# Normalizing x tile by tile between attention slots, in a fused attention and gating kernel

## The chip, the cores and the metric

The kernel runs on one core of one Trainium2 chip. The metric is the device time of one execution in microseconds (us). Most executions agree within about 0.3%. Here the spread follows the mean clock that the chip granted to TensorE: in the 33 runs of the kernel before whose clock is on record, those at a mean clock of 0.989 to 0.991 of full speed (16 runs) had spans of 1152.2 to 1155.2 us, those at 0.994 to 0.996 (17 runs) had 1147.5 to 1150.8 us. Traces are therefore compared at equal clock where possible (all traced executions had 0.994 to 0.998), and some means below are over runs at a clock of 0.994 or more.

## The reference

```python
x = A_x                                  # 1 x 2048 x 640, bf16
xn = _layernorm(x)                       # (x - mean) / sqrt(var + eps)
s = attention(xn @ wq, k_cache[..., -512:, :], v_cache[..., -512:, :]) @ wo   # 32 heads of 192
# B: the two tokens with the largest r = xn @ w_r go through a small gated MLP,
#    scaled by sigmoid(r); the result is added to their rows of xn
g = silu(xn + scatter(y))
return x + s * g
```

The work is nearly all attention: 32 heads, 2048 queries, 512 keys. LayerNorm stands before everything, and the router (`r` for all 2048 tokens, then the best two) and the MLP of two tokens are small.

## The kernel before

The 32 heads are worked off in 16 pairs, and each pair in four slots of 512 queries. 2048 tokens are 16 tiles of 128 rows. `load_pair` starts the loads of one pair's keys, values and weights on the sync queue. First all 16 tiles of x are loaded, then all statistics are taken, then all tiles are normalized and transposed (`xnT` is what the q projection and the router read):

```python
x_all = lnp.tile([P, NT, D], BF16, name="x_all")
for t in range(NT):
    eng = nc.sync if t % 2 == 0 else nc.gpsimd
    eng.dma_start(out=x_all[:, t, :], in_=x2[t * P:(t + 1) * P, :])
loaded[0] = load_pair(0)
for t in range(NT):
    ...  # bn_stats, bn_aggr -> mv_all[:, t, :]
...      # rstd_all = 1 / sqrt(var + eps), one Sqrt for all tiles
for t in range(NT):
    nc.vector.tensor_scalar(out=xn_all[:, t, :], in0=x_all[:, t, :], scalar1=mv_all[:, t, 0:1],
                            scalar2=rstd_all[:, t:t + 1], op0=ALU.subtract, op1=ALU.mult)
    for d0 in range(0, DT, 4):
        ...
        pst = ps_a.tile([P, 4, P], BF16, name="pst", tag="ps_a")        # ps_a: two PSUM buffers
        for dt in range(dn):
            nc.tensor.transpose(pst[:, dt, :], xn_all[:, t, ...], ident[:])
        nc.any.tensor_copy(out=xnT[:, d0:d0 + dn, t * P:(t + 1) * P], in_=pst[:, :dn, :])
```

The router and the MLP are stages that are hung into the slots of attention, one stage a slot. Stage 1 is the router: 20 matmuls, then a chain of single-row operations on VectorE.

```python
def b_stage1():
    ...  # r_ps[1, 512] = wr_col^T @ xnT, 4 x 5 matmuls, copied to r_row
    r_bf = bw.tile([1, S], BF16, name="r_bf")
    nc.vector.tensor_copy(out=r_bf[:], in_=r_row[:])
    r_rt = bw.tile([1, S], F32, name="r_rt", tag="rowB")
    nc.vector.tensor_copy(out=r_rt[:], in_=r_bf[:])
    nc.vector.max(out=mx8[:], in_=r_rt[:])
    nc.vector.max_index(out=idx8[:], in_max=mx8[:], in_values=r_rt[:])
    ...
# stage 2: one-hot selectors E and ET; 3: the two rows; 4: gate and up (w_c, 24 loads); 5: down (wd_c)
def b_stage_g(c):                       # 16 of these, four a slot
    g_ps = ps_y.tile([P, 2, 512], F32, name="y_ps2")
    for nh in range(2):
        nc.tensor.matmul(g_ps[:, nh, :NH], lhsT=ident_h[:], rhs=xn_all[:, c, ...], start=True, stop=False)
        nc.tensor.matmul(g_ps[:, nh, :NH], lhsT=B.ET[:, c * P:(c + 1) * P], rhs=B.y_sb[:, ...],
                         start=False, stop=True)
    ...  # tanh on ScalarE, g = (tanh + 1) * g_ps on VectorE, written over xn_all

for i, st in enumerate(stages):
    b_sched.setdefault(slots[min(i, len(slots) - 1)], []).append(st)
```

Of the kernel before, what the change touches and what calls it, by code (L numbers as in the profile page):

```python
# [11 lines left out]
F32 = mybir.dt.float32  # L12
BF16 = mybir.dt.bfloat16
U32 = mybir.dt.uint32
I32 = mybir.dt.int32
# [4 lines left out]
def kernel(  # L20
# [15 lines left out]
    nc = tc.nc  # L36
    P = 128
    _, S, D = A_x.shape
# [5 lines left out]
    NT = S // P  # L44
# [4 lines left out]
    NQC = S // QC  # L49
    QPC = QC // P  # L50
# [7 lines left out]
    x2 = A_x[0]  # L58
    out2 = out[0]

    const = ctx.enter_context(tc.tile_pool(name="const", bufs=1))
# [10 lines left out]
    xn_all = big.tile([P, NT, D], BF16, name="xn_all")  # L72
# [44 lines left out]

    loaded = {}

    with tc.tile_pool(name="ln", bufs=1) as lnp, tc.tile_pool(name="lns", bufs=4) as lns:  # L120
        FMAX = nc.vector.BN_STATS_FMAX
        nch = (D + FMAX - 1) // FMAX
        while D % nch != 0:
            nch += 1
        csz = D // nch
        x_all = lnp.tile([P, NT, D], BF16, name="x_all")
        mv_all = lnp.tile([P, NT, nc.vector.BN_AGGR_DIM], F32, name="mv_all")
        for t in range(NT):
            eng = nc.sync if t % 2 == 0 else nc.gpsimd
            eng.dma_start(out=x_all[:, t, :], in_=x2[t * P:(t + 1) * P, :])  # L130
        loaded[0] = load_pair(0)
        for t in range(NT):
            stats = lns.tile([P, nch, nc.vector.BN_STATS_DIM], F32, name="stats")
            for c in range(nch):
                nc.vector.bn_stats(out=stats[:, c, :], in_=x_all[:, t, c * csz:(c + 1) * csz])
            nc.vector.bn_aggr(out=mv_all[:, t, :], in_=stats[:])
        rstd_all = lnp.tile([P, NT], F32, name="rstd_all")
        nc.vector.tensor_scalar_add(out=rstd_all[:], in0=mv_all[:, :, 1], scalar1=EPS)
        nc.scalar.activation(out=rstd_all[:], in_=rstd_all[:], func=ACT.Sqrt)
        nc.vector.reciprocal(out=rstd_all[:], in_=rstd_all[:])  # L140
        for t in range(NT):
            nc.vector.tensor_scalar(out=xn_all[:, t, :], in0=x_all[:, t, :], scalar1=mv_all[:, t, 0:1],
                                    scalar2=rstd_all[:, t:t + 1], op0=ALU.subtract, op1=ALU.mult)
            for d0 in range(0, DT, 4):
                dn = min(4, DT - d0)
                pst = ps_a.tile([P, 4, P], BF16, name="pst", tag="ps_a")
                for dt in range(dn):
                    nc.tensor.transpose(pst[:, dt, :], xn_all[:, t, (d0 + dt) * P:(d0 + dt + 1) * P], ident[:])
                nc.any.tensor_copy(out=xnT[:, d0:d0 + dn, t * P:(t + 1) * P], in_=pst[:, :dn, :])

    bw = ctx.enter_context(tc.tile_pool(name="bw", bufs=1))
    bs = ctx.enter_context(tc.tile_pool(name="bs", bufs=3))
# [3 lines left out]
    B = _NS()  # L156
# [3 lines left out]
    def b_stage1():  # L160
        wr_col = bw.tile([P, DT], BF16, name="wr_col")
        with nc.allow_non_contiguous_dma(reason="tiny router weight load"):
            nc.gpsimd.dma_start(out=wr_col[:], in_=B_w_r.rearrange("(dt p) -> p dt", p=P))
        r_row = bw.tile([1, S], F32, name="r_row", tag="rowA")
        RC = 512
        for c0 in range(0, S, RC):
            cw = min(RC, S - c0)
            r_ps = ps_a.tile([1, RC], F32, name="r_ps", tag="ps_a")
            for dt in range(DT):
                nc.tensor.matmul(r_ps[:, :cw], lhsT=wr_col[:, dt:dt + 1], rhs=xnT[:, dt, c0:c0 + cw],  # L170
                                 start=(dt == 0), stop=(dt == DT - 1))
            nc.vector.tensor_copy(out=r_row[:, c0:c0 + cw], in_=r_ps[:, :cw])
        r_bf = bw.tile([1, S], BF16, name="r_bf")
        nc.vector.tensor_copy(out=r_bf[:], in_=r_row[:])
        r_rt = bw.tile([1, S], F32, name="r_rt", tag="rowB")
        nc.vector.tensor_copy(out=r_rt[:], in_=r_bf[:])
        mx8 = bw.tile([1, 8], F32, name="mx8")
        nc.vector.max(out=mx8[:], in_=r_rt[:])
        idx8 = bw.tile([1, 8], U32, name="idx8")
        nc.vector.max_index(out=idx8[:], in_max=mx8[:], in_values=r_rt[:])  # L180
        B.sel = bw.tile([1, 4], F32, name="sel")
        nc.vector.tensor_copy(out=B.sel[:, 0:2], in_=idx8[:, 0:2])
        nc.vector.tensor_copy(out=B.sel[:, 2:4], in_=mx8[:, 0:2])
        iota_tok_i = bw.tile([P, NT], I32, name="iota_tok_i")
        nc.gpsimd.iota(iota_tok_i[:], pattern=[[P, NT]], base=0, channel_multiplier=1)
        B.iota_tok = bw.tile([P, NT], F32, name="iota_tok")
        nc.vector.tensor_copy(out=B.iota_tok[:], in_=iota_tok_i[:])

    def b_stage2():
        sel = B.sel  # L190
        selb_ps = ps_a.tile([P, 4], F32, name="selb_ps", tag="ps_a")
        nc.tensor.matmul(selb_ps[:], lhsT=ones_f[:, :], rhs=sel[:], start=True, stop=True)
        selb = bw.tile([P, 4], F32, name="selb")
        nc.vector.tensor_copy(out=selb[:], in_=selb_ps[:])
        selT_ps = ps_a.tile([2, 2], F32, name="selT_ps", tag="ps_a")
        for j in range(2):
            nc.tensor.matmul(selT_ps[:, j:j + 1], lhsT=sel[:, 2 * j:2 * j + 2], rhs=ones_f[:, 0:1],
                             start=True, stop=True)
        selT = bw.tile([2, 2], F32, name="selT")
        nc.vector.tensor_copy(out=selT[:], in_=selT_ps[:])  # L200
        B.sig = bw.tile([2, 1], F32, name="sig")
        nc.scalar.activation(out=B.sig[:], in_=selT[:, 1:2], func=ACT.Exp, scale=-1.0)
        nc.vector.tensor_scalar_add(out=B.sig[:], in0=B.sig[:], scalar1=1.0)
        nc.vector.reciprocal(out=B.sig[:], in_=B.sig[:])
        B.E = bw.tile([P, NT, 2], BF16, name="E")
        for j in range(2):
            nc.vector.tensor_scalar(out=B.E[:, :, j], in0=B.iota_tok[:], scalar1=selb[:, j:j + 1],
                                    scalar2=None, op0=ALU.is_equal)
        iota_row_i = bw.tile([2, S], I32, name="iota_row_i", tag="rowA")
        nc.gpsimd.iota(iota_row_i[:], pattern=[[1, S]], base=0, channel_multiplier=0)  # L210
        iota_row = bw.tile([2, S], F32, name="iota_row", tag="rowB")
        nc.vector.tensor_copy(out=iota_row[:], in_=iota_row_i[:])
        B.ET = bw.tile([2, S], BF16, name="ET")
        nc.vector.tensor_scalar(out=B.ET[:], in0=iota_row[:], scalar1=selT[:, 0:1], scalar2=0.5,
                                op0=ALU.is_equal, op1=ALU.mult)
# [42 lines left out]
    def b_stage_g(c):  # L258
        g_ps = ps_y.tile([P, 2, 512], F32, name="y_ps2")
        for nh in range(2):  # L260
            nc.tensor.matmul(g_ps[:, nh, :NH], lhsT=ident_h[:], rhs=xn_all[:, c, nh * NH:(nh + 1) * NH],
                             start=True, stop=False)
            nc.tensor.matmul(g_ps[:, nh, :NH], lhsT=B.ET[:, c * P:(c + 1) * P], rhs=B.y_sb[:, nh * NH:(nh + 1) * NH],
                             start=False, stop=True)
        th = bs.tile([P, 2, NH], F32, name="th", tag="bs")
        nc.scalar.activation(out=th[:], in_=g_ps[:, :, :NH], func=ACT.Tanh)
        nc.vector.scalar_tensor_tensor(out=xn_all[:, c, :].rearrange("p (a n) -> p a n", a=2),
                                       in0=th[:], scalar=1.0, in1=g_ps[:, :, :NH],
                                       op0=ALU.add, op1=ALU.mult)

    b_sched = {}
    slots = [(pi_, qc_) for pi_ in range(NPAIR) for qc_ in range(NQC)]
    stages = [b_stage1, b_stage2, b_stage3, b_stage4, b_stage5]
    GPS = 4
    for c0 in range(0, NT, GPS):
        stages.append(lambda c0=c0: [b_stage_g(c) for c in range(c0, min(NT, c0 + GPS))])
    for i, st in enumerate(stages):
        b_sched.setdefault(slots[min(i, len(slots) - 1)], []).append(st)

    g_all = xn_all  # L280

# [104 lines left out]
    for t in range(NT):  # L386
        x_t = bs.tile([P, D], BF16, name="x_f", tag="bs")
# [35 lines left out]
```

## Time and profile before

| | before |
|---|---|
| time | 1151.54 us median of 4 (1148.92 to 1155.28) |
| TensorE busy | 94% |
| first transpose of x | 19.82 us |
| first q matmul | 45.52 us |
| first softmax exponential | 53.94 us |

The head of the page of the kernel before. PE is TensorE, PEld its weight loads, DVE VectorE, ACT ScalarE, POOL GpSimd; each has busy time, share of the span and number of instructions.

```profile
span 1148.6 us, 19485 instructions
PE 1083.4 (94%) x7178; PEld 587.9 (51%) x7178; DVE 885.8 (77%) x2189; ACT 745.0 (65%) x1718; POOL 52.3 (5%) x85
```

The Trainium skill ("Trainium Kernel Development and Optimization", Performance Expectations, the paragraph on reading a trace) warns that busy time of matmuls is a bad metric for the distance to the limit, and names the busy share of weight loads as one of two good ones.

The timeline of TensorE before, from 12 us on. Columns: start, duration, engine, line, operation, output and inputs, shape, count, and in brackets the idle time before it with what ended it. A count over 1 merges a run of equal instructions.

```profile
19.82 0.72 PE L148 MATMUL pst<-ident,xn_all 128*128 128x128 bf16 x5 [19.82 <-DVE xn_all L142]
21.10 0.69 PE L148 MATMUL pst<-ident,xn_all 128*128 128x128 bf16 x5 [0.57 <-ACT xnT L149]
...
36.13 0.69 PE L148 MATMUL pst<-ident,xn_all 128*128 128x128 bf16 x5 [0.32 <-DVE xnT L149]
37.14 1.69 PE L315 MATMUL kT_ps<-ident,k_p 128*128 128x128 bf16 x12 [0.32 <-DVE xnT L149]
39.41 6.17 PE L170 MATMUL r_ps<-xnT,wr_col 128*1 128x512 bf16 x20 [0.58 <-ACT kT_p L322]
45.52 1.68 PE L334 MATMUL q_ps<-xnT,wq_p 128*128 128x512 bf16 x7
```

Sixteen tiles are transposed at one tile in 1.0 to 1.3 us, each waiting for a copy out of PSUM; then come the key transposes, the router, and only at 45.5 us attention. The router's chain on VectorE then holds the first softmax back. The VectorE timeline before:

```profile
46.33 1.21 DVE L174 CAST r_bf<-r_row 1x2048 bf16<-1x2048 f32 x1
47.58 2.94 DVE L176 CAST r_rt<-r_bf 1x2048 f32<-1x2048 bf16 x1
51.04 2.27 DVE L178 MAX8 mx<-r_rt 1x8 f32<-1x2048 f32 x1
53.90 2.27 DVE L180 FIND_INDEX8 idx<-mx,r_rt 1x8 uint32<-1x2048 f32 x1
```

and the table of windows before (window, its length, busy time and count of each engine, granted TensorE clock, DMA share, GB/s):

```profile
50.00:55.00 5.00, 0.84 (x3) 0.32 (x4) 5.00 (x6) 1.64 (x3) 0.00 (x0) 0.81 0.00 0
55.00:60.00 5.00, 3.54 (x19) 1.86 (x18) 4.98 (x15) 2.14 (x5) 0.00 (x0) 0.50 0.00 0
```

VectorE is busy for all ten microseconds, TensorE for 0.84 of the first five, and its clock then falls to half.

### The profile page before, as it was taken

Reading aid. Unit: us, or ns where it says so; the run is one execution under the profiler, and the core shown is the slowest. Engines: PE = TensorE matmul, PEld = TensorE weight load, DVE = VectorE, ACT = ScalarE, POOL = GpSimd, SP = SyncE. Lnnn points to the kernel's source line nnn. Section 1 sums busy time; section 2 is a strip of 40 time slices with the busy share of each in tenths; the row PEclk is TensorE's granted clock in tenths of the full one; section 3 lists DMA queues with packets and bytes.
Section 4 is the critical chain, followed back from the end, with each engine's and each line's share of the span. In section 5 each row is a group of like instructions: output and inputs, shape, how many; then the busy total and the mean of one; then the engine's idle time right before and its main releaser. Section 6 shows DMA issues by size and latency. Waiting matters only on the chain.

```text
span 1148.6 us, 19485 instructions
## 1 busy us (share of the span) xinstructions
PE 1083.4 (94%) x7178; PEld 587.9 (51%) x7178; DVE 885.8 (77%) x2189; ACT 745.0 (65%) x1718; POOL 52.3 (5%) x85
## 2 busy tenths in 40 slices
PE   1698999999999999999999999999999999999995
PEld 1354345644565545654555545654456545655553
DVE  7577687688966887678865988568865989568996
ACT  2376576478855877478854878458854878458662
POOL 3005300000000000000000000000000000000000
PEclk9989999999999999999999999999999999999999
DMA  9105301021011101012011101112020200010022
GB/s 213 34 1 135 100 17 30 1 59 29 18 29 36 32 15 37 10 37 44 17 30 36 32 15 24 22 36 45 2 45 13 54 15 18 15 41 1 25 69 80
DMA packets 125119, 43.33 MB, mean 38 GB/s; under 512 B 111968, under 2 KB 123232, under 8 KB 125024
## 3 DMA queue, kind: packets, MB, share of 16 engines
q1 hardware_dynamic: 122496, 34.88, 13.6%
q0 software_dynamic: 2528, 7.21, 2.3%
q8 instruction: 56, 0.92, 0.3%
q14 instruction: 39, 0.32, 0.1%
HBM read 39.45 MB, written 2.62 MB: 37 GB/s over the span
## 4 chain that ended last, share of the span: by engine, by line
PE 69%; ACT 10%; issue 8%; DVE 7%; DMA 3%; SPq 2%; POOL 1%; ACTq 0%; DVEq 0%; POOLq 0%
PE o_ps L369 17%; PE y_ps L291 16%; PE q_ps L334 12%; PE pT_ps L362 8%; PE s_ps L348 8%; PE s_ps L349 7%; ACT p_sb L354 6%; DVE nmx L351 3%; ACT pT L364 2%; ACT oT_p L371 1%; DMA w_c<-in_B_w_up_dram 1%; DVE diag L359 1%; DVE acc L299 1%; DMA wd_c<-in_B_w_down_dram 1%; DMA w_c<-in_B_w_gate_dram 1%
## 5 line engine op out<-in xcount | busy, mean ns | idle before, releaser
L354 ACT ACTIVATE p_sb<-s_ps,nmx 128x512 bf16<-128x512 f32 x512 | 352.0, 689 | 101.3 <-DVE nmx L351 84.8
L351 DVE TENSOR_REDUCE nmx<-s_ps 128x1 f32<-128x512 f32 x512 | 347.2, 683 | 32.1 <-PE s_ps L349 25.0
L334 PE MATMUL q_ps<-xnT,wq_p 128*128 128x512 bf16 x960 | 280.6, 380 | 0.0
L369 PE MATMUL o_ps<-pT,v_p 128*128 128x512 bf16 x1024 | 263.3, 378 | 2.8 <-ACT oT_p L371 0.8
L291 PE MATMUL y_ps<-wo_p,oT_p 128*128 128x320 bf16 x1536 | 241.3, 299 | 4.7 <-DVE acc L299 4.0
L364 ACT CAST pT<-pT_ps 128x512 bf16<-128x512 f32 x312 | 182.1, 584 | 92.6 <-PE pT_ps L362 89.7
L362 PEld LDWEIGHTS <-p_sb 128*128 128x128 bf16 x2048 | 151.3, 98 | 133.7 <-issue 28.7
L362 PE MATMUL pT_ps<-diag,p_sb 128*128 128x128 bf16 x2048 | 200.6, 219 | 8.0 <-DVE diag L359 3.9
L348 PE MATMUL s_ps<-kT_p,qT_p 128*128 128x512 bf16 x512 | 194.2, 380 | 9.0 <-ACT p_sb L354 5.0
L349 PE MATMUL s_ps<-kT_p,qT_p 128*128 128x512 bf16 x512 | 194.6, 380 | 1.8 <-DVE qT_p L337 1.8
L291 PEld LDWEIGHTS <-oT_p 128*128 128x128 bf16 x1536 | 148.2, 98 | 81.3 <-issue 6.0
L371 ACT CAST oT_p<-o_ps 64x512 bf16<-64x512 f32 (+1 forms) x181 | 105.3, 582 | 122.2 <-PE o_ps L369 121.3
L299 DVE TENSOR_TENSOR acc<-acc,y_ps 128x640 f32<-128x640 f32 x112 | 91.7, 818 | 108.6 <-PE y_ps L291 107.2
L369 PEld LDWEIGHTS <-v_p 128*128 128x128 bf16 x1024 | 98.5, 97 | 125.8 <-issue 30.1
L364 DVE CAST pT<-pT_ps 128x512 bf16<-128x512 f32 x200 | 137.6, 688 | 23.8 <-PE pT_ps L362 19.2
L359 DVE TENSOR_SCALAR diag<-ident,rr 128x128 bf16<-128x128 bf16 x512 | 128.7, 253 | 7.9
L334 PEld LDWEIGHTS <-wq_p 128*128 128x128 bf16 x960 | 87.4, 98 | 66.7 <-issue 1.0
L357 DVE RECIPROCAL rr<-rs 128x1 f32<-128x1 f32 x512 | 79.7, 157 | 33.8 <-ACT p_sb L354 27.5
L339 ACT ACTIVATE qT_p<-q_ps 128x512 bf16<-128x512 f32 x128 | 76.5, 598 | 42.0 <-PE q_ps L334 41.0
L354 ACT ACTIVATION_READ_ACCUMULATOR p_sb<-s_ps,nmx 128x1 f32 x512 | 102.0, 199 | 0.0
L349 PEld LDWEIGHTS <-qT_p 128*128 128x128 bf16 x512 | 49.7, 97 | 55.1 <-issue 33.2
L348 PEld LDWEIGHTS <-qT_p 128*128 128x128 bf16 x512 | 50.2, 98 | 24.1 <-issue 0.3
(82 smaller groups left out, 413.9 us busy)
## 6 DMA issues: line engine op xcount, KB each, us to landing
wq_p<-in_A_wq_dram SPq DMA_DIRECT2D x32, 160.0 KB, 2.8
wo_p<-in_A_wo_dram SPq DMA_DIRECT2D x32, 160.0 KB, 2.4
k_p<-in_A_k_cache_dram SPq DMA_DIRECT2D x32, 128.0 KB, 2.5
v_p<-in_A_v_cache_dram SPq DMA_DIRECT2D x32, 128.0 KB, 2.6
wq_p<-in_A_wq_dram SPq DMA_DIRECT2D x32, 80.0 KB, 2.8
wo_p<-in_A_wo_dram SPq DMA_DIRECT2D x32, 80.0 KB, 2.3
x_f<-in_A_x_dram SPq DMA_DIRECT2D x16, 160.0 KB, 2.2
out_dram<-o_t SPq DMA_DIRECT2D x16, 160.0 KB, 1.8
```

The lines of the kernel that those rows point to most:

```text
L291: nc.tensor.matmul(y_ps2[:, nh, :NH], lhsT=oT_g[:, b, ts_], rhs=wo_g[:, b, nh * NH:(nh + 1) * NH], start=(i == 0), stop=(i == nmm - 1))
L299: nc.vector.tensor_tensor(out=acc_v, in0=acc_v, in1=y_ps2[:, :, :NH], op=ALU.add)
L334: nc.tensor.matmul(q_ps[:], lhsT=wq_p[:, dt, b, :], rhs=xnT[:, dt, q0:q0 + QC], start=(dt == 0), stop=(dt == DT - 1))
L348: nc.tensor.matmul(s_ps[:], lhsT=qT_p[:, bq, qs], rhs=kT_p[:, 3 * hh, :], start=True, stop=False)
L349: nc.tensor.matmul(s_ps[:], lhsT=qT_p[:, 1, qs], rhs=kT_p[:, 1 + hh, :], start=False, stop=True)
L351: nc.vector.tensor_reduce(out=nmx[:], in_=s_ps[:], axis=AX.X, op=ALU.max, negate=True)
L354: nc.scalar.activation(out=p_sb[:], in_=s_ps[:], func=ACT.Exp, bias=nmx[:], scale=1.0, accum_out=rs[:])
L359: nc.vector.tensor_scalar_mul(out=diag[:], in0=ident[:], scalar1=rr[:])
L362: nc.tensor.matmul(pT_ps[:, kt, :], lhsT=p_sb[:, kt * P:(kt + 1) * P], rhs=diag[:], start=True, stop=True)
L364: nc.any.tensor_copy(out=pT[:, :, qs], in_=pT_ps[:])
L369: nc.tensor.matmul(o_ps[:], lhsT=v_p[:, kt, b, :], rhs=pT[:, kt, :], start=(kt == 0), stop=(kt == KT - 1))
L371: nc.any.tensor_copy(out=oT_p[rows, b, q0:q0 + QC], in_=o_ps[rows, :])
```

## The change

Its intent: attention needs only the first four normalized tiles to begin. So each slot of the first pair normalizes its own four tiles, the router and all later stages move three slots back, and two integer-to-float casts of iota rows go. The normalize step is now outside the pool that held x, so it loads x once more.

```diff
+    mv_all = const.tile([P, NT, nc.vector.BN_AGGR_DIM], F32, name="mv_all")
+    rstd_all = const.tile([P, NT], F32, name="rstd_all")
     ...
-        for t in range(NT):
-            nc.vector.tensor_scalar(out=xn_all[:, t, :], in0=x_all[:, t, :], scalar1=mv_all[:, t, 0:1],
+    def ln_stage(tiles):
+        for t in tiles:
+            x_t = bs.tile([P, D], BF16, name="x_ln", tag="bs")          # bs: three buffers
+            nc.sync.dma_start(out=x_t[:], in_=x2[t * P:(t + 1) * P, :])
+            nc.vector.tensor_scalar(out=xn_all[:, t, :], in0=x_t[:], scalar1=mv_all[:, t, 0:1],
                                     scalar2=rstd_all[:, t:t + 1], op0=ALU.subtract, op1=ALU.mult)
     ...
-        r_rt = bw.tile([1, S], F32, name="r_rt", tag="rowB")
+        r_rt = r_row
     ...
-        iota_tok_i = ...; nc.gpsimd.iota(iota_tok_i[:], ...)             # int32
-        nc.vector.tensor_copy(out=B.iota_tok[:], in_=iota_tok_i[:])
+        nc.gpsimd.iota(B.iota_tok[:], ..., allow_small_or_imprecise_dtypes=True)
     ...  # the same for iota_row [2, 2048]
+    for k in range(NQC):
+        b_sched.setdefault(slots[min(k, len(slots) - 1)], []).append(
+            lambda k=k: ln_stage(range(k * QPC, (k + 1) * QPC)))
     for i, st in enumerate(stages):
-        b_sched.setdefault(slots[min(i, len(slots) - 1)], []).append(st)
+        b_sched.setdefault(slots[min(i + NQC - 1, len(slots) - 1)], []).append(st)
```

More of the change, by code (lines that the diff above doesn't have):

```diff
@@ L126 @@
         x_all = lnp.tile([P, NT, D], BF16, name="x_all")
-        mv_all = lnp.tile([P, NT, nc.vector.BN_AGGR_DIM], F32, name="mv_all")
         for t in range(NT):
@@ L136 @@
             nc.vector.bn_aggr(out=mv_all[:, t, :], in_=stats[:])
-        rstd_all = lnp.tile([P, NT], F32, name="rstd_all")
         nc.vector.tensor_scalar_add(out=rstd_all[:], in0=mv_all[:, :, 1], scalar1=EPS)
@@ L183, in b_stage1 @@
         nc.vector.tensor_copy(out=B.sel[:, 2:4], in_=mx8[:, 0:2])
-        iota_tok_i = bw.tile([P, NT], I32, name="iota_tok_i")
-        nc.gpsimd.iota(iota_tok_i[:], pattern=[[P, NT]], base=0, channel_multiplier=1)
         B.iota_tok = bw.tile([P, NT], F32, name="iota_tok")
-        nc.vector.tensor_copy(out=B.iota_tok[:], in_=iota_tok_i[:])
+        nc.gpsimd.iota(B.iota_tok[:], pattern=[[P, NT]], base=0, channel_multiplier=1,
+                       allow_small_or_imprecise_dtypes=True)
     def b_stage2():
@@ L208, in b_stage2 @@
                                     scalar2=None, op0=ALU.is_equal)
-        iota_row_i = bw.tile([2, S], I32, name="iota_row_i", tag="rowA")
-        nc.gpsimd.iota(iota_row_i[:], pattern=[[1, S]], base=0, channel_multiplier=0)
-        iota_row = bw.tile([2, S], F32, name="iota_row", tag="rowB")
-        nc.vector.tensor_copy(out=iota_row[:], in_=iota_row_i[:])
+        iota_row = bw.tile([2, S], F32, name="iota_row", tag="rowA")
+        nc.gpsimd.iota(iota_row[:], pattern=[[1, S]], base=0, channel_multiplier=0,
+                       allow_small_or_imprecise_dtypes=True)
         B.ET = bw.tile([2, S], BF16, name="ET")
```

## The prediction

> **What bounds the kernel now.** The page of the kernel before has the span at 1148.6 us: TensorE busy 1083.4 us (94%), VectorE 885.8 us (77%), ScalarE 745.0 us (65%). From 63 us on TensorE streams 128x512 matmuls every 0.215 us and waits little. In the timeline the first transpose is at 19.8 us and the first q matmul at 45.5 us. Full flow begins only at 63 us.
>
> **What the start consists of.** Statistics on VectorE end at 18.5 us. Normalize plus 80 transposes take 19.3 to 37 us at 1.0 us a tile, a ping-pong of TensorE (0.69), ScalarE copy (0.59) and VectorE copy (0.23) over two PSUM buffers. K transposes follow to 38.8 us, router matmuls to 45.5 us, at half clock (0.43 us each until 43 us). VectorE's router chain (casts 1.2 and 2.9, max 2.3, index 2.3 us) then holds up the first softmax: TensorE waits 1.8, 3.0 and 1.4 us and falls back to half clock (granted clock 0.66 in 50:60). The Trainium skill, "TensorE: Matmul & The Clock Gate", Part 1, states about 3.4 us of sustained work to warm up; the trace agrees (39.4 to about 43 us).
>
> **What the change does.** Only four tiles must now be normalized before attention starts, and the router moves three slots later. But normalize reads x again, in three shared buffers, and these loads stand in the sync queue behind both pair loads. In the trace that queue issues its 32nd pair load at 28.2 us. I expect the first reload issued at about 27 us (three gate-weight loads no longer compete), landing at 29 to 30 us, the fourth tile, which waits for a buffer, at about 33 us, and the first q matmul at about 35 us: 10 us earlier.
>
> **What it gives back.** At that moment 60 transposes (60 x 0.056 = 3.4 us warm) and 20 router matmuls (4.3 us) are still to be done, where VectorE and ScalarE are nearly as full. Per slot of four tiles they gain about 4.7 us between them, some 2.3 us each; three slots make up to 7 us. The first 15 q matmuls run cold (about +2 us). The router chain, which before was hidden partly in the start-up wait, now interrupts running attention (about 8 us of VectorE, 4 to 5 us lost by TensorE). The dropped casts save 1.4 us and about 1.7 us in the r_rt cast, which overlapped an iota.
>
> The waits for gate, up and down weights (6.6 us on TensorE in 63:187) move with their stages and remain. The wo projection still starts right after pair 1, the g stages after it in pair 2. VectorE gets about 22 more 64-row output copies (0.69 us each), ScalarE as many fewer.
>
> **Sum:** -10 (start) +3.4 +4.3 +2 +4 (router, more stalls) -3 (casts) -4 (start-up waits filled with deferred work) = about -3 us, with schedule noise of several us.
>
> **Predicted:** 1148 us, range 1137 to 1160. Chances: faster by over 2% 0.03, within 2% 0.94, slower by over 2% 0.03.
>
> **Right if:** first q matmul near 35 us; first x reload issued 26 to 29 us; a dip in TensorE and clock near the end of pair 0; the third pair's K load about where it was (107 us, +-5). **Wrong if:** reloads are issued much earlier or later; deferred work fills idle time wholly (then 8 to 10 us gained); or the 0.69 us copies moved to VectorE slow the steady state.

## More of the kernel before

The order of instructions within each engine is laid out by a scheduler when the kernel is built; the program text fixes the dependences, not the exact order.

## The result

The changed kernel took 1149.65 us (median of 10 runs, 1148.52 to 1155.32), the kernel before 1151.93 us (median of 15, 1148.92 to 1156.01). The ratio is 0.9987 with a 95% interval of 0.9969 to 1.0004: the same. Ratios in this document are the mean time of one kernel's fast runs over that of the other's fast runs of the same rounds, so not quite the ratio of the medians quoted.

The head of the page after, whose shares answer to those of before:

```profile
span 1147.4 us, 19540 instructions
PE 1081.2 (94%) x7178; PEld 585.4 (51%) x7178; DVE 890.9 (78%) x2203; ACT 736.3 (64%) x1703; POOL 52.1 (5%) x85
```

The timeline of TensorE after:

```profile
17.85 0.61 PE L320 MATMUL kT_ps<-ident,k_p 128*128 128x128 bf16 x4 [1.55 <-DMA k_p<-in_A_k_cache_dram]
30.65 0.71 PE L152 MATMUL pst<-ident,xn_all 128*128 128x128 bf16 x5 [12.19 <-DVE xn_all L146]
...
33.94 0.69 PE L152 MATMUL pst<-ident,xn_all 128*128 128x128 bf16 x5 [0.57 <-ACT xnT L153]
35.20 5.32 PE L339 MATMUL q_ps<-xnT,wq_p 128*128 128x512 bf16 x15 [0.57 <-DMA k_p<-in_A_k_cache_dram]
...
41.22 0.44 PE L152 MATMUL pst<-ident,xn_all 128*128 128x128 bf16 x5
42.28 0.44 PE L152 MATMUL pst<-ident,xn_all 128*128 128x128 bf16 x5 [0.62 <-ACT xnT L153]
```

The key transposes now come first, only four tiles are transposed before the first q matmul, and that stands at 35.20 us, 10.3 us earlier. (The view puts the last wait, 0.57 us, down to a key load, which a q matmul does not read; what it needed was the copy of the fourth tile, which ended on ScalarE at 35.15 us.) The deferred transposes reappear inside attention, from 41.22 us on. What set the new start is the reload of x. The sync queue after (the queue's own issues, L110 to L115 are the pair loads, L145 the reload) and then VectorE after:

```profile
25.77 0.50 SPq L115 DMA_DIRECT2D wo_p<-in_A_wo_dram  x1
26.65 1.29 SPq L145 DMA_DIRECT2D x_ln<-in_A_x_dram  x3
```

```profile
25.16 0.25 DVE L140 RECIPROCAL rstd_all<-rstd_all 128x16 f32<-128x16 f32 x1 [0.28 <-ACT rstd_all L139]
30.14 1.24 DVE L146 TENSOR_SCALAR xn_all<-x_ln,mv_all,rstd_all 128x640 bf16<-128x640 bf16 x3 [4.73 <-DMA x_ln<-in_A_x_dram]
```

The statistics are ready at 25.4 us, and VectorE then idles 4.73 us for data that it had held in memory a moment before. The 16 reloads of 160 KB took 2.0 to 3.4 us from issue to landing, 2.4 us in the median. The Trainium skill ("DMA: Bandwidth & Descriptors", Anatomy of one DMA) gives about 2.0 us plus the bytes at 436 GB/s for loads issued by GpSimd, an estimate of 2.4 us for this size; these loads are issued from the sync queue, and the trace agrees all the same.

The router's chain is now at 90 to 100 us, inside running attention. VectorE after:

```profile
89.93 1.22 DVE L178 CAST r_bf<-r_row 1x2048 bf16<-1x2048 f32 x1
91.17 1.22 DVE L180 CAST r_row<-r_bf 1x2048 f32<-1x2048 bf16 x1
92.95 2.27 DVE L182 MAX8 mx<-r_row 1x8 f32<-1x2048 f32 x1
95.81 2.27 DVE L184 FIND_INDEX8 idx<-mx,r_row 1x8 uint32<-1x2048 f32 x1
98.14 1.87 DVE L186 CAST sel<-idx 1x2 f32<-1x2 uint32 x1
```

and the windows after:

```profile
96.00:100.00 4.00, 0.93 (x6) 0.41 (x6) 4.00 (x8) 0.70 (x2) 1.83 (x1) 1.00 0.86 160
100.00:104.00 4.00, 3.43 (x19) 1.86 (x19) 1.74 (x12) 2.71 (x7) 0.00 (x0) 0.57 0.01 1
```

It is the same hold-up as before, moved: TensorE works 0.93 of 4 us and then runs at a clock of 0.57. (The last cast, of two elements, takes 1.87 us because GpSimd writes an iota row of 1.83 us at the same moment, from 98.16 us on; in the kernel before it was the `r_rt` cast, 2.94 us instead of 1.22, that lay over an iota of 1.82 us from 47.61 us on. The Trainium skill, "SBUF — State Buffer", SBUF: two separate sides, says of the port pair that VectorE and GpSimd share that it is an exclusive lock, which GpSimd or a VectorE operation in a two-port mode holds for a whole instruction while the other is blocked. The lengths agree with that: each cast is longer by 1.72 or 1.73 us, nearly the length of the iota. In which mode the casts ran, and which side held the lock, the trace does not show; each cast's record starts 0.02 to 0.03 us before the iota's.)

### Where the lead of 10 us went

The kernel executes 512 softmax exponentials, always in the same order, so the start of the n-th, counted from 0, is a mark for comparing kernels. The differences below are computed from the ScalarE timelines; negative means that the changed kernel is ahead. The 64th is the end of the second pair, the 96th the end of the third, by which both kernels have done all router, MLP and g work.

| n | 0 | 8 | 24 | 64 | 80 | 96 | 128 | 320 | end of span |
|---|---|---|---|---|---|---|---|---|---|
| after minus before, us | -10.4 | -15.6 | -6.0 | -16.0 | -10.0 | +2.0 | +3.6 | +4.9 | -1.1 |

How far single traces can be compared is shown by the second trace of the changed kernel (`after_again` below). Its 7178 matmuls stand in the same order as in the first, but its marks are 1.5 to 1.6 us later from the 64th on: from 45 to 49 us its granted clock was 0.57, and 1.00 in the first trace. A difference of less than about 1.6 us between two traces is therefore not read as an effect of a change.

Between the first q matmul and the 96th exponential both kernels do the same attention, MLP and g work on TensorE, but the changed kernel does more besides. An account of TensorE in that stretch, each matmul counted from its start to the next one's start:

| from first q matmul to 96th exponential | before | after |
|---|---|---|
| from, to | 45.5 to 271.8 us | 35.2 to 273.8 us |
| length | 226.3 us | 238.6 us |
| deferred transposes (60) | none | 8.7 us |
| router matmuls (20) | none | 4.9 us |
| all the rest | 226.3 us | 225.0 us |

So 12.3 us more, of which 13.6 us are the two deferred items; and that is the lead of 10.3 us and another 2.0. A second thing happens later: from the 96th exponential to the end the kernel before needed 876.7 us and the changed one 873.6 us, although the text of that part is the same. Both points are taken up below.

Theory T: from the first q matmul on, TensorE's own in-order time decides. The change started attention 10 us earlier by moving 13.6 us of TensorE work behind the start, and so could gain nothing. Rival A: the lead was still there at the 64th exponential and was lost in the third pair, because g stages and the output projection share one PSUM buffer and now meet there. Rival B: VectorE and ScalarE pay for the deferred normalizing and copying. Rival C: the start is masked by later loads, so an earlier start is worth nothing.

### The profile page after: what moved, and what is told of

Its sections match the earlier page's. It is cut to its first block, busy times and chain, and to the rows that moved or that the text cites. A ratio compares the mean times of both kernels' runs of the same rounds, so it can differ in the third digit from the quotient of the medians.

```text
span 1147.4 us, 19540 instructions
## 1 busy us (share of the span) xinstructions
PE 1081.2 (94%) x7178; PEld 585.4 (51%) x7178; DVE 890.9 (78%) x2203; ACT 736.3 (64%) x1703; POOL 52.1 (5%) x85
## 4 chain that ended last, share of the span: by engine, by line
PE 64%; ACT 7%; DVE 4%; issue 2%; ACTq 0%
PE o_ps L374 16%; PE y_ps L296 14%; PE q_ps L339 11%; PE pT_ps L367 8%; PE s_ps L353 8%; PE s_ps L354 6%; ACT p_sb L359 4%; ACT oT_p L376 2%; DVE nmx L356 1%; ACT pT L369 1%; DVE acc L304 1%; DVE diag L364 1%; PE kT_ps L320 0%; DVE rr L362 0%; ACT qT_p L344 0%
## 5 line engine op out<-in xcount | busy, mean ns | idle before, releaser
L339 PE MATMUL q_ps<-xnT,wq_p 128*128 128x512 bf16 x960 | 285.1, 382 | 0.6 <-DMA k_p<-in_A_k_cache_dram 0.6
L369 ACT CAST pT<-pT_ps 128x512 bf16<-128x512 f32 x320 | 186.8, 584 | 100.7 <-PE pT_ps L367 98.1
L376 ACT CAST oT_p<-o_ps 128x512 bf16<-128x512 f32 (+1 forms) x161 | 93.7, 582 | 108.4 <-PE o_ps L374 107.7
L369 DVE CAST pT<-pT_ps 128x512 bf16<-128x512 f32 x192 | 132.1, 688 | 22.6 <-PE pT_ps L367 17.8
L364 DVE TENSOR_SCALAR diag<-ident,rr 128x128 bf16<-128x128 bf16 x512 | 131.0, 258 | 7.5
L376 DVE CAST oT_p<-o_ps 64x512 bf16<-64x512 f32 (+1 forms) x95 | 65.5, 689 | 12.9 <-PE o_ps L374 12.8
L354 PEld LDWEIGHTS <-qT_p 128*128 128x128 bf16 x512 | 49.8, 97 | 49.4 <-issue 26.0
```

What stands on the lines that cost most here:

```text
L339: nc.tensor.matmul(q_ps[:], lhsT=wq_p[:, dt, b, :], rhs=xnT[:, dt, q0:q0 + QC], start=(dt == 0), stop=(dt == DT - 1))
L354: nc.tensor.matmul(s_ps[:], lhsT=qT_p[:, 1, qs], rhs=kT_p[:, 1 + hh, :], start=False, stop=True)
L364: nc.vector.tensor_scalar_mul(out=diag[:], in0=ident[:], scalar1=rr[:])
L369: nc.any.tensor_copy(out=pT[:, :, qs], in_=pT_ps[:])
L376: nc.any.tensor_copy(out=oT_p[rows, b, q0:q0 + QC], in_=o_ps[rows, :])
```

## The experiments

All outputs are right.

### One half of the change at a time

`iota_only` is the kernel before with the casts dropped; `defer_only` has the deferral and keeps the casts.

```diff
 # iota_only, against before
-        r_rt = bw.tile([1, S], F32, name="r_rt", tag="rowB")
+        r_rt = r_row
-        (int32 iota tiles and their casts)
+        (float iotas)
 # defer_only, against before: mv_all, rstd_all, ln_stage and the two lines of the schedule of the change
```

> The kernel before with only the iota part of the change (float iota written directly, the bf16 round trip of the router row written in place; LayerNorm stays in front). Theory T (from the first q matmul on, TensorE's own time is what counts; the change moved 8.7 us of transposes and 4.9 us of router matmuls behind that point and so spent the 10.3 us by which q starts earlier): VectorE loses 1.4 us of casts, and the 2.9 us cast is no longer stretched by an overlapping iota; this lies in the stretch where TensorE waits for the first softmax, so 1 to 3 us faster, about 0.998 of before. Rival (the casts are hidden): within 0.5 us of before. Neither expects the whole change's effect to come from here.

> The changed kernel with the iota part undone (integer iota and casts as before, separate router row). Theory T: the router chain now sits at the end of head pair 0 where TensorE waits about 3 us for it; the extra cast of 1.2 us and a router cast stretched by the overlapping iota lengthen that wait, so 1 to 3 us slower than the changed kernel, i.e. about equal to the kernel before (0.999 to 1.002). Rival (the deferral alone gives the gain): same as the changed kernel within 0.5 us.

Measured: `iota_only` 1154.33 us, ratio 1.001 (0.9985 to 1.0036); `defer_only` 1151.94 us, ratio 0.9975 (0.9952 to 0.9997); the kernel before had 1155.53 us in these rounds. Dropping the casts alone shows no gain (the interval leaves room for at most 1.7 us). The `r_rt` cast fell from 2.94 to 1.22 us as it should. But the float iota now takes the buffer of `r_row`, so it can start only after the index search, and it then ran beside the cast of `sel`, which took 1.87 us instead of 0.14: the stall moved to another cast. The maximum search started 0.8 us earlier than before and the end did not move. The expectation of 1 to 3 us was a miss.

The deferral alone cannot be told from the whole change by its ratio. Part of that ratio is clock, though: 7 of the 11 runs of the kernel before in these rounds had a clock of 0.991 or less, and at 0.994 or more its mean is 1151.6 us (4 runs), that of `defer_only` 1152.0 (6 runs). In the traces the 96th exponential of `defer_only` was 3.4 us later than that of the changed kernel, but the 64th only 0.4; the rest came with granted clocks of 0.61 and 0.54 in 256:260 and 260:264, after a wait of 1.02 us at 256.8 us that the changed kernel has too and passed at a clock of 1.00. So whether the casts save something beside the deferral is open.

### No reload: x normalized in place

```diff
 # inplace, against after
-        x_all = lnp.tile([P, NT, D], BF16, name="x_all")
+        x_all = xn_all
-            x_t = bs.tile([P, D], BF16, name="x_ln", tag="bs")
-            nc.sync.dma_start(out=x_t[:], in_=x2[t * P:(t + 1) * P, :])
-            nc.vector.tensor_scalar(out=xn_all[:, t, :], in0=x_t[:], ...
+            nc.vector.tensor_scalar(out=xn_all[:, t, :], in0=xn_all[:, t, :], ...
```

> The changed kernel without the second read of x: x is loaded straight into the buffer that holds the normalized rows, and normalized in place. Theory T: VectorE has the reciprocal root ready at about 25 us, so the first q matmul moves from 35.2 us to 29 to 31 us and, as TensorE's work afterwards is the same, the end moves with it: 4 to 6 us faster than the changed kernel, about 1144 to 1146 us. Rival A (the lead is lost in head pair 2, where the g stages and the wo projection share one PSUM buffer, whatever the start): q earlier by the same 5 us, but the end unchanged within 1 us.

Measured: 1149.78 us, ratio 0.9957 (0.9933 to 0.9981). The first q matmul came at 31.32 us instead of 35.20, and the first exponential 4.3 us earlier. But the gain was 2.8 us after the router chain (24th) and 0.4 us from the 64th on. The trace shows where the last part went. TensorE and windows of `inplace`:

```profile
139.88 0.28 PE L235 MATMUL y_ps<-xselT,w_c 128*128 128x2 bf16 x5 [1.91 <-DMA w_c<-in_B_w_gate_dram]
```

```profile
139.00:142.00 3.00, 2.12 (x18) 1.25 (x19) 0.69 (x1) 0.66 (x2) 0.87 (x1) 0.70 0.10 35
142.00:145.00 3.00, 3.00 (x23) 1.47 (x22) 1.27 (x5) 1.58 (x5) 1.38 (x2) 0.73 0.39 109
```

A gate weight, which waits for one of three shared buffers, landed late; TensorE idled 1.91 us and then ran at half clock until about 143.6 us (the lost clock of the two windows adds up to 3.4 us at half speed). The changed kernel waited 0.36 us at the same matmul and kept its clock. So 4.3 us of T's 4 to 6 us were had at the start and mostly lost to one late load (3.7 us ahead at the 32nd, 0.4 at the 64th). This is what rival C says, in one case; whether it holds in general is tested below. The timing does not settle the remaining gain: the changed kernel was not run in these rounds.

### The g stages spread out

```diff
 # g_spread, against after
-    GPS = 4
-    for c0 in range(0, NT, GPS):
-        stages.append(lambda c0=c0: [b_stage_g(c) for c in range(c0, min(NT, c0 + GPS))])
+    for c in range(NT):
+        b_sched.setdefault(slots[16 + 2 * c], []).append(lambda c=c: b_stage_g(c))
```

> The changed kernel with the 16 g stages taken out of slots 8 to 11 (head pair 2) and put one into every second slot from slot 16 (pairs 4 to 11). Theory T: the lead of 16 us at the 64th softmax lasts longer (still some 12 us at the 96th), but each g stage costs TensorE the same 0.95 us wherever it stands, so the end is within 2 us of the changed kernel. Rival A (collision of g and wo on the one PSUM buffer in pair 2 eats the lead): 6 to 12 us faster than the changed kernel at the end.

Measured: 1150.78 us, ratio 0.9969 (0.9947 to 0.9991), span 1148.5. Against the changed kernel the lead at the 96th exponential was 14.5 us, at the 224th 8.3, at the 320th 5.2 and at the 480th 0.5: each g stage costs TensorE about 1 us wherever it stands. Rival A falls. It was only the order of the work that made the lead appear and vanish: twelve of the 16 g stages ran in the second pair before, all 16 in the third after.

### Work added on one engine

`more_pe` transposes the 12 deferred tiles four times instead of once (180 more transposes into the same PSUM tiles); `more_dve` normalizes each of them twice more into an unused tile (24 more VectorE operations, 10.5 us).

```diff
 # more_pe, against after
-                    nc.tensor.transpose(pst[:, dt, :], xn_all[...], ident[:])
+                    for _rep in range(4 if t >= QPC else 1):
+                        nc.tensor.transpose(pst[:, dt, :], xn_all[...], ident[:])
 # more_dve, against after
+            if t >= QPC:
+                for _rep in range(2):
+                    junk = bw.tile([P, D], BF16, name="junk")
+                    nc.vector.tensor_scalar(out=junk[:], in0=xn_all[:, t, :], ...)
```

> The changed kernel once more, to compare the kernels of this set with it on one chip. Every theory: 0.996 to 1.001 of the kernel before, as on its first run (0.9987).

> The changed kernel with each of the 60 deferred transposes of the token tiles 4 to 15 done four times over into the same PSUM place (180 more on TensorE, nothing else added). Theory T (TensorE's time after the first q matmul is what counts): 180 x 0.056 to 0.062 us = 10 to 11 us slower than the changed kernel. Rival B (the deferred work is paid on VectorE and ScalarE, which do the normalize and the copies): at most 3 us slower.

> The changed kernel with two unread normalizes more for each of the token tiles 4 to 15 (24 more VectorE instructions of 0.44 us, 10.5 us in the same slots; TensorE's list unchanged). Theory T: at most 3 us slower than the changed kernel. Rival B (VectorE is what the deferred work is paid on): 7 to 11 us slower.

Measured, in the same rounds (before 1151.46 us): the changed kernel again 1149.83, ratio 0.9973 (0.9954 to 0.9993); `more_pe` 1157.85, ratio 1.0047 (1.0027 to 1.0067); `more_dve` 1151.35, ratio 0.999 (0.997 to 1.001). In the account of TensorE the deferred transposes rose from 8.7 to 18.5 us, and the lag against the first trace of the changed kernel was 8.9 us at the 24th exponential and 8.2 to 8.3 us at the marks from the 96th to the 504th (against its second trace 6.6 to 6.8; the medians are 8.0 us apart). That is less than the 10 to 11 us expected. 10.5 us of VectorE cost 1.2 us at the 96th and 1.7 us at the 511th (against the second trace nothing; the medians are 1.5 us apart). So T holds in the main and rival B falls: most of the work added on TensorE reaches the end and is never won back, work on VectorE hardly counts.

The account also shows why 60 transposes cost 8.7 us at 145 ns each, when 180 more cost only 9.85 us, 55 ns each: the transposes as such are cheap, but a tile's five transposes wait for the copies out of two shared PSUM buffers (the 0.62 us wait at 42.28 us above).

### Four matmuls in another order

The g stage alternates a stationary operand of 128 rows (`ident_h`) with one of 2 rows (`ET`). The timelines of TensorE and of its weight loads after:

```profile
253.69 0.30 PE L263 MATMUL y_ps<-xn_all,ident_h 128*128 128x320 bf16 x1
253.92 0.30 PE L265 MATMUL y_ps<-y_sb,ET 2*128 2x320 bf16 x1
254.15 0.31 PE L263 MATMUL y_ps<-xn_all,ident_h 128*128 128x320 bf16 x1
254.40 0.30 PE L265 MATMUL y_ps<-y_sb,ET 2*128 2x320 bf16 x1
```

```profile
253.91 0.09 PEld L265 LDWEIGHTS <-ET 2*128 2x128 bf16 x1 [0.18 <-issue]
254.15 0.10 PEld L263 LDWEIGHTS <-ident_h 128*128 128x128 bf16 x1
254.39 0.09 PEld L265 LDWEIGHTS <-ET 2*128 2x128 bf16 x1
```

The matmuls start 0.23 to 0.25 us apart, while output projections of the same width (320 columns, 128 rows) start 0.137 us apart. The difference, about 0.1 us, is the length of one weight load. In this sequence each load starts 0.22 us or more after the start of the matmul before it, and within 0.01 us of its own matmul. For comparison, a stretch of TensorE after in which every stationary operand has 128 rows:

```profile
700.52 1.03 PE L374 MATMUL o_ps<-pT,v_p 128*128 128x512 bf16 x4
701.38 0.39 PE L367 MATMUL pT_ps<-diag,p_sb 128*128 128x128 bf16 x4
701.61 0.38 PE L339 MATMUL q_ps<-xnT,wq_p 128*128 128x512 bf16 x1
```

Four 512-column matmuls take 0.86 us and four 128-column ones 0.23 us from start to start, each with a weight load of its own, and none of these loads shows: that of the first 512-column matmul starts at 700.30 us, 0.22 us ahead of it. The experiment puts equal row counts side by side:

```diff
 # g_reorder, against after
     for nh in range(2):
         nc.tensor.matmul(g_ps[:, nh, :NH], lhsT=ident_h[:], ...)
+    for nh in range(2):
         nc.tensor.matmul(g_ps[:, nh, :NH], lhsT=B.ET[:, c * P:(c + 1) * P], ...)
```

> The changed kernel with the four matmuls of a g stage ordered so that the two with the 128-row identity come first and the two with the 2-row selector after them, where they alternated (0.235 us each against 0.137 us for matmuls of the same width in the wo projection). Same work and same engines. If the alternation costs the difference, half of it goes: 2 to 4 us of TensorE time in 16 stages; theory T says the end moves by the same 2 to 4 us, rival A and B say it does not move (within 1 us).

Measured: 1146.6 us, ratio 0.995 (0.993 to 0.9971). The order of instructions is otherwise that of the changed kernel. TensorE of `g_reorder`:

```profile
251.33 0.43 PE L263 MATMUL y_ps<-xn_all,ident_h 128*128 128x320 bf16 x2
251.70 0.44 PE L266 MATMUL y_ps<-y_sb,ET 2*128 2x320 bf16 x2
252.07 0.34 PE L368 MATMUL pT_ps<-diag,p_sb 128*128 128x128 bf16 x3
```

Two matmuls now take 0.37 us from the first's start to the next pair's, 0.187 us each instead of 0.235. Within this run, a matmul with the same number of rows as the one before it follows after 0.135 to 0.147 us in all 16 g tiles (identity after identity, selector after selector); where the rows change, the next one follows after 0.226 to 0.232 us (31 of 32 times; once 0.35). So it is the change of rows that costs, 0.08 to 0.1 us each time; the last identity and the first selector write different halves of the PSUM tile, so it is not two matmuls adding into the same place. The changed kernel was 3.4 us behind at the 96th exponential and at every mark after it; 3.1 us of this came between the 64th and the 96th, where the g stages lie (the medians are 3.2 us apart). This saving on TensorE counts in full.

### An earlier start

If T is right, work must leave the stretch before the first q matmul without entering the one behind it. The reload, and statistics of 12 tiles that attention does not yet need, do that: `early` loads the first four tiles first, takes their statistics and their square root alone, normalizes in place, transposes them before the keys, and takes the other 12 tiles' statistics afterwards.

```diff
 # early, against after
+    load_x(range(0, QPC, 2), nc.sync); load_x(range(1, NT, 2), nc.gpsimd)
+    loaded[0] = load_pair(0, mid=lambda: load_x(range(QPC, NT, 2), nc.sync))   # mid: after keys and wq
     ...                                                                        # x goes into xn_all
-            x_t = bs.tile([P, D], BF16, name="x_ln", tag="bs")                 # no reload
-            nc.sync.dma_start(out=x_t[:], in_=x2[t * P:(t + 1) * P, :])
     ...
-    for k in range(NQC):
+    for k in range(1, NQC):
     ...
+        if pi == 0:
+            ln_stats(range(QPC)); ln_stage(range(QPC)); ln_stats(range(QPC, NT))
+            (the key copies of this pair go to ScalarE)
 # early_g: and the order of g_reorder
 # early_g_w: and six buffers of their own for the gate, up and down weights
+    wst = ctx.enter_context(tc.tile_pool(name="wst", bufs=6))
-            w_c = bs.tile([P, DT, P], BF16, name="w_c", tag="bs")
+            w_c = wst.tile([P, DT, P], BF16, name="w_c", tag="wst")             # wd_c alike
 # early_g_w_r: and the router row copied and cast by ScalarE
-            nc.vector.tensor_copy(out=r_row[:, c0:c0 + cw], in_=r_ps[:, :cw])
-        nc.vector.tensor_copy(out=r_bf[:], in_=r_row[:])
+            nc.scalar.copy(out=r_bf[:, c0:c0 + cw], in_=r_ps[:, :cw])
-        nc.vector.tensor_copy(out=r_rt[:], in_=r_bf[:])
+        nc.scalar.copy(out=r_rt[:], in_=r_bf[:])
```

> No reload of x; the first four tiles of x are loaded first, get statistics of their own, and are normalized and transposed before the key transposes, whose copies go to ScalarE. Theory T (from the first query matmul on, TensorE's own in-order time decides, so an earlier start is worth its microseconds in full): first query matmul at 15 to 21 us instead of 35.2, and the end 10 to 16 us earlier than in the changed kernel, near 1134 to 1139 us, less 1 to 4 us if late gate-weight loads hold TensorE as they did when x was normalized in place. Rival theory (the start is masked: something later, the loads of weights or of the next pair's keys, sets the pace): the lead is there at the first exponentials and gone by the 128th, and the end moves by less than 4 us.

> As the early start, with the four matmuls of each g tile ordered identity, identity, ET, ET. Theory T: a further 3 to 4 us less, as the reordering alone gave in the changed kernel; the g matmuls at about 0.19 us rather than 0.235. Rival theory: the saving is swallowed by the next wait, and the two runs are within 1 us.

> As the one before, with the gate, up and down weights in six buffers of their own instead of the three shared ones. If the late gate-weight load costs TensorE about 2 us of idle and some more at a halved clock, as it did in the run that normalized in place, this gives 1 to 4 us and the granted clock of 0.5 to 0.6 in that stretch is gone. If that loss came from something else, within 1 us.

> As the one before, with the router row copied and cast by ScalarE, so that two single-partition VectorE casts of about 1.2 us each leave the chain at the end of the first pair. If that chain holds TensorE, 1 to 4 us less and a shorter wait of TensorE there; if ScalarE's own queue then holds the softmax instead, no gain or up to 2 us more.

Measured, beside 1151.97 us for the kernel before:

| | time, median | ratio to before (95%) | span of the trace |
|---|---|---|---|
| early | 1140.34 us | 0.989 (0.9871 to 0.9909) | 1139.5 us |
| early_g | 1137.74 us | 0.9878 (0.9855 to 0.99) | 1133.9 us |
| early_g_w | 1134.48 us | 0.9837 (0.9819 to 0.9856) | 1132.9 us |
| early_g_w_r | 1131.62 us | 0.9812 (0.9795 to 0.983) | 1130.0 us |

TensorE of `early`:

```profile
17.30 0.71 PE L161 MATMUL pst<-ident,xn_all 128*128 128x128 bf16 x5 [17.30 <-DVE xn_all L155]
...
24.69 5.12 PE L353 MATMUL q_ps<-xnT,wq_p 128*128 128x512 bf16 x15 [0.48 <-ACT kT_p L341]
```

The first q matmul came at 24.69 us: 10.5 us earlier than in the changed kernel, though not at the 15 to 21 us expected, because the first normalized tile was ready only at 17.3 us. The end came 7.9 us earlier in the trace, where 10 to 16 less 1 to 4 were expected.

Clock enters these ratios too. The means of the runs at a clock of 0.994 or more are 1151.4 us (before, 6 of 11 runs), 1140.1 (`early`, 5 of 6), 1137.1 (`early_g`, 4 of 6), 1134.5 (`early_g_w`, 5 of 5) and 1131.6 (`early_g_w_r`, 5 of 5): about 3 us a step. By the ratios alone `early_g` cannot be told from `early`, and its trace below is that of its fastest run, so the 5.6 us between the two traces are more than the kernels differ by. The marks, each kernel against the one before it in the list:

| n | 0 | 8 | 24 | 64 | 96 | 128 | 320 | 511 | span |
|---|---|---|---|---|---|---|---|---|---|
| early minus after, us | -10.7 | -11.0 | -10.9 | -7.8 | -7.8 | -7.8 | -7.7 | -7.9 | -7.9 |
| early_g minus early | +1.0 | +1.0 | +1.0 | -2.5 | -5.6 | -5.6 | -5.6 | -5.6 | -5.6 |
| early_g_w minus early_g | -0.3 | -0.2 | -0.2 | +4.6 | -3.8 | -3.4 | -6.8 | +0.6 | -1.0 |
| early_g_w_r minus early_g_w | +0.5 | +0.5 | +2.3 | -0.6 | -0.8 | -0.8 | +2.5 | -4.5 | -2.9 |

The first row is the strongest evidence for T and against rival C. An earlier start stays in hand through the router chain, loses 3.1 us in one place between the 24th and the 64th, and is then kept within 0.2 us until the end. The one loss is again a late gate weight, for which the changed kernel waited only 0.36 us: the waits of TensorE in `early` between 112 and 170 us (engine, what waited, for what: total, times, longest), and the windows after the wait:

```profile
PE y_ps L246 <- DMA w_c<-in_B_w_gate_dram: 2.2, 2, 2.0
PE y_ps L264 <- DMA wd_c<-in_B_w_down_dram: 1.4, 2, 1.0
```

```profile
130.00:133.00 3.00, 1.03 (x13) 0.54 (x12) 1.29 (x2) 0.60 (x1) 0.50 (x1) 1.00 0.52 138
133.00:136.00 3.00, 3.00 (x21) 1.33 (x18) 1.11 (x3) 1.93 (x5) 1.74 (x2) 0.67 0.21 57
136.00:139.00 3.00, 3.00 (x28) 1.73 (x26) 1.95 (x4) 0.99 (x2) 1.69 (x2) 0.76 0.34 76
```

In `early_g` the same wait happened to be 1.3 us long, and the clock stayed at 1.00. That accounts for part of its first 3.5 us (between the 24th and the 64th); the other 3.1 us came in the stretch of the g stages, as expected of the reordering. With buffers of their own (`early_g_w`) six of the 24 gate and up weights were there about 100 us ahead, where it had been three, and the others landed 0.1 to 2.1 us before their use; 0.3 us of waiting for a down weight is all that is left of these waits, and TensorE was busy all 20 us from 120 to 140. (The +4.6 at the 64th is again a matter of order: TensorE did side work sooner that the other kernel did after this mark.) That was 3.8 us by the 96th exponential. The router row on ScalarE is not shown to help: the 24th exponential came 2.3 us later and the 96th 0.8 us earlier, since the two casts on ScalarE (the last one 1.90 us) delay the same chain that they were to shorten. The 2.9 us of its span come mostly from the next point.

### What the scheduler did with the unchanged part

From the 96th exponential to the end of the span, all kernels have the same work in the program text (save `g_spread`, whose g stages lie there). The traces fall into two groups:

| from the 96th exponential to the end | us |
|---|---|
| before, iota_only, early_g_w | 876.7, 876.7, 876.3 |
| after, after_again, defer_only, inplace, g_reorder | 873.6, 873.9, 874.0, 874.0, 873.7 |
| more_pe, more_dve, early, early_g, early_g_w_r | 873.9, 874.1, 873.5, 873.5, 874.3 |

The order of TensorE's instructions in the built programs explains the groups as far as it goes: in the first, pairs take 62.6 and 68.5 us in turn, in the second 65.9 and 64.9 (between the exponentials at pair boundaries, from the sixth pair on), with output projections standing at other places between the q matmuls. Behind the 96th exponential q matmuls occupied 241 ns each, from start to start, in the three traces of the first group and 236 or 237 ns in the ten of the second. From the 192nd to the 256th exponential the order of the 848 matmuls is the same within each group and differs between the groups. It is not the clock, which was 0.998 to 1.000 in this part in all 13. The scheduler lays these pairs out differently depending on what came before. So about 3 us of the changed kernel's time are a side effect of the layout; it came with the deferral (`defer_only` has it, `iota_only` does not), but is not what the deferral was meant to do. No run forced one layout on another kernel's text, so this is shown by the grouping of 13 traces, not by an experiment; which detail of the layout costs the 3 us is open.

## Why the prediction was right

The total was right, 1148 us predicted and 1149.65 measured, and the class too. Most steps were, but two errors partly cancelled, and that was luck.

- **Right: the start.** First q matmul at 35.20 us (predicted about 35), first reload issued at 26.65 us (about 27), first normalize at 30.14 (29 to 30), fourth tile, which waits for a buffer, normalized at 33.15 (about 33). The lead was 10.3 us (10).
- **Right: the first q matmuls run cold.** Fifteen took 5.3 us (4.5 in the second trace); at 0.215 us each they would have taken 3.2, so +2.1 (+2).
- **Right: the router's matmuls.** 4.9 us (4.3); its hold-up at the end of the first pair, with the clock at 0.57, is there.
- **Mis-sized: "60 transposes (60 x 0.056 = 3.4 us warm)".** They occupied 8.7 us. The prediction took the spacing of 128-column matmuls in an unbroken stream; a transpose here also waits for its PSUM buffer, and TensorE is in order, so the wait is paid by whatever stands behind it. `more_pe` confirmed it: transposes without an extra buffer cost 55 ns each.
- **Wrong in its worth: "-3 (casts)".** `iota_only` showed no effect. What the prediction missed: the stall beside the iota did not go with the `r_rt` cast but moved to the cast of `sel`, 1.87 us here as in `iota_only`. The other small terms of the sum (+2 cold, +4 router stalls, -4 waits filled, -3 casts: together -1) came to -1.3 together in the account (-0.7 in the second trace); how that splits was not measured.
- **Missing: the layout.** The 3.1 us that the part behind the 96th exponential became shorter are in no term. The prediction had named "schedule noise of several us".
- **Wrong: "the third pair's K load about where it was (107 us, +-5)".** It was issued at 96.4 us. The lead was still 11 us there and was lost only in the third pair, when all 16 g stages came due. The prediction looked for the loss too early.

Put together from the traces: -10.3 (start) +8.7 (transposes) +4.9 (router) -1.3 (rest) = +2.0 us at the 96th exponential, and -3.1 (layout) makes -1.1 us, which is the difference of the spans, 1148.56 and 1147.44. The prediction's -3 contained a transposes term 5.3 us too small and lacked a term of -3.1, for which it had only "schedule noise of several us": that the sign came out right is luck. On the quantity that it set out to reason about, the deferral, the change lost 2 us (3.4 in the second trace).

## What to carry to other kernels

When one engine is in order and nearly always streaming, starting its main flow earlier gains only what leaves its queue for good, or what filled a wait: move work of other engines and loads ahead of the start, not its own work behind it. Cost a deferred operation by its spacing where it will stand, with the wait for its buffer, not by its spacing in an unbroken stream; and watch a mark such as the n-th softmax over the whole run, because a lead that comes and goes may be only the order in which the same work is done. Trace one kernel twice before reading small differences: here the same program differed by 1.5 us, with the clock. Before crediting a change with a few microseconds, check whether the scheduler also rearranged the part that was not changed.

## What the Trainium skill lacked or had wrong

- "TensorE: Matmul & The Clock Gate", Back-to-back issue gap: it gives a sustained spacing of about 81 ns for 128 columns and 131 ns for 512 in a stream of weight loads and matmuls, and calls N/2.4 + 2.5 ns an under-count at 128 and an over-count at 512 columns. In this kernel's streams every matmul has its own weight load (7178 of each on the profile's page), and the stretch of the kernel after shown with the reordered matmuls has four 512-column matmuls in 0.86 us and four 128-column ones in 0.23 us, 215 and 57 ns each: the formula is right here and the two sustained figures are not.
- The same page, The mechanism: its list says that weight loads overlap with running matmuls only when the row group differs, though the text above it names a background weight buffer as well. Here loads of 128 rows following 128 rows are hidden (0.135 us per 320-column matmul), and a change between 128 and 2 rows exposes the load: 0.226 to 0.232 us at a change in `g_reorder`, 0.135 to 0.147 without. The page gives no cost of alternating row counts.
- The same page, What's actually happening: it says that the clock halves after an idle window of about 3.4 us. Here waits of 1.9 and 2.0 us were followed by half clock (0.70 and 0.73; 0.67 and 0.76 in windows of 3 us), in a stretch of which some matmuls have only two columns; a wait of 1.3 us in the same place was not. One wait of 1.02 us was followed by it in `defer_only` (0.61 and 0.54 in windows of 4 us) and the same wait was not in the changed kernel (1.00). The page does not say how little work makes a window an idle one; its section on a second failure mode tells of short idle times that did the same in another kernel, without their length.
- I found no page that warns of the build's scheduler laying out an unchanged part of a kernel differently: 873.5 to 874.3 us against 876.3 to 876.7 here for the same work.
